# Gathering the 1/den sums and the second LN's ones matmuls into one block of column-tiled matmuls

## The chip, the cores and the metric

One NeuronCore of a Trainium2 chip runs the whole program. The metric is the device time of one execution in microseconds. Profiles are one execution each; their times count from the span's start, and the span is some 1.8 us shorter than the device time.

## The reference, cut to what matters

A conditioned transformer block: a layer norm with shift and scale, linear attention, a second layer norm with shift and scale, and a gated FFN. The change touches the denominator of the attention and the shift and scale of the second norm.

```python
mod = (_silu(c) @ w_mod).reshape(c.shape[0], 6, 1, -1)      # sa, ca, ga, sb, cb, gb
h = _layernorm(x) * (1 + ca) + sa
# linear attention, 32 heads of 32, 2048 tokens
z   = einsum('bhsd->bhd', pk)
num = einsum('bhqd,bhde->bhqe', pq, kv)
den = einsum('bhqd,bhd->bhq', pq, z)[..., None] + 1e-06
o   = num / den
x = x + ga * (o @ wo)
h = _layernorm(x) * (1 + cb) + sb                           # <- sb, cb
x = x + gb * (gelu(h @ w_gate) * (h @ w_up) @ w_down)
```

## The kernel before

The kernel records operations into one list per engine, with semaphores derived from the ranges they touch; VectorE, ScalarE and GpSimd are reordered by a small scheduler in one stretch, TensorE and the sync engine's transfers stay in program order.

The parts that matter: the denominator sums write 32 partitions each, four matmuls side by side; so do the ones matmuls that broadcast a row of modulation values.

```python
def den(pr_, b):                       # one token half: 8 groups x 4 column tiles
    for g in range(NG):
        for i in range(4):
            e.matmul(ps_all[32*i:32*(i+1), b*512:b*512+HW], Z32[:, g, :], PQ[sg][:, g, t0:t0+HW], ...)
    # VectorE: RDC = PSUM + 1e-6, RDC = 1/RDC;  store(): RDC -> scr_rd in HBM

def mod_pass():                        # second LN's shift and scale
    mod_rows(((2, 4, 5, hl_src),))     # 8 ones matmuls, 32 partitions each, into PSUM bank 5
    o_r = mod_store(4, 5, MROW[1], ...)            # ScalarE copy, store to scr_row in HBM
    for dst, nt, a0 in ((SBT, "sbT", 0), (CBT, "cbT", 2)):
        # load scr_row by column: 1024 elements of 4 bytes each
        e.dma_start(dst[:, :], scr_row[1, a0:a0+2, :].rearrange("a (b p) -> p (a b)", p=P))

# what runs after which key-times-x tile (m_tile) of the attention tail
HOOK = {..., 14: "w2 modp", 15: "kv3 z32", 16: "den0", 17: "w3", 18: "rb0.0",
        19: "kv4 den1", 20: "w4 rb0.1", ...}
```

1/den comes back from HBM as `rb`, broadcast over partitions, 1 MB for each half of a group of 512 tokens. Each chunk of 128 tokens is then normalised by ScalarE and GpSimd for the second norm (`ln2_a`: sum, squares, normalise) and transposed by a DMA.

```python
def xh_buf(c_):
    i = c_ % 3                         # three buffers: chunk 3 reuses chunk 0's
    return XH[i], r_2k(XHO[i], f"xh{i}")

for c_ in range(3, 12):
    ...
    if c_ == 4:
        pq_scale(1, 1, GH[0] + GH[1])
        rb_load(3, (0,))               # first half of the last reload, 1 MB
    wo_chunk(c_, 2 * (c_ % 4))
    ...
    if c_ in (4, 5, 6):
        ln2_a(c_ - 3, False)           # chunks 1 to 3, each with its transpose to h2T
```

## Time and profile before

| | before |
|---|---|
| device time, median of the 3 runs | 833.59 us (833.45 to 833.72) |
| TensorE busy | 99% of the span |
| first key-times-x tile starts | 126.97 us |
| first FFN matmul starts | 234.45 us |
| last addition starts | 829.47 us |

The last three rows are read from the timeline of TensorE and the chain by time (start, length, engine, line, what):

```profile
126.97 1.18 PE L826 MATMUL ps_all<-xrow,pk 128*128 128x341 bf16 x7
234.45 0.38 PE L1325 MATMUL ps_all<-h2T,wg 128*128 128x512 bf16 x1
829.47 0.22 DVE xall L1360
```

They cut the execution in three: a start-up of 127 us, a middle of 107.48 us that holds everything the change touches on TensorE, and an FFN of 595.02 us.

### The profile page before, as it was taken

The numbers are of one execution on the slowest core, as the hardware profiler recorded it, in microseconds if no ns is written. First come the engines' busy times: TensorE is split into PE (matmuls) and PEld (weight loads), VectorE is DVE, ScalarE is ACT, GpSimd is POOL, SyncE is SP. The second block draws the span as 40 slices with busy tenths as digits, with TensorE's granted clock in tenths as the row PEclk, the third lists the DMA queues.
The fourth block names the chain that finished last, engine by engine and source line by source line (L and its number), as shares of the span: only waits on it lengthen the run. The fifth ranks groups of instructions, "written<-read, shape, count | busy, mean of one in ns | idle before, by whom it ended". The sixth has DMA issues, their size and how long they took to land.

```text
span 831.7 us, 11593 instructions
## 1 busy us (share of the span) xinstructions
PE 826.5 (99%) x4253; PEld 392.3 (47%) x4253; DVE 509.9 (61%) x920; ACT 321.1 (39%) x542; POOL 35.5 (4%) x90
## 2 busy tenths in 40 slices
PE   8999999999999999999999999999999999999998
PEld 4444446665444444444444444444444444444445
DVE  6799888834777577753555565355556535555522
ACT  2597642323523354410444441044444104444300
POOL 2122100000200000000000000000000000000000
DMA  9798769368998788070555533055553306555000
GB/s 286 233 187 220 164 138 262 58 128 196 228 273 240 228 249 256 34 170 19 160 152 152 151 102 76 20 162 154 154 145 102 76 20 170 155 153 137 7 20 26
DMA packets 216929, 121.90 MB, mean 147 GB/s; under 512 B 69276, under 2 KB 206756, under 8 KB 215848
## 3 DMA queue, kind: packets, MB, share of 16 engines
q1 hardware_dynamic: 216856, 121.16, 55.9%
q8 instruction: 34, 0.56, 0.3%
q14 instruction: 23, 0.19, 0.1%
q10 hardware_dynamic: 16, 0.00, 0.0%
HBM read 103.03 MB, written 4.47 MB: 129 GB/s over the span
## 4 chain that ended last, share of the span: by engine, by line
PE 97%; SPq 2%; DMA 1%; issue 0%; DVE 0%
PE ps_all L1353 23%; PE ps_all L1328 23%; PE ps_all L1325 23%; PE ps_all L826 7%; PE ps_all L862 7%; PE ps_all L1189 7%; PE ps_all L811 5%; SPq L568 1%; DMA wmq<-in_w_mod_dram 1%; SPq L573 1%; PE ps_all L844 0%; PE ps_all L1121 0%; PE ps_all L1148 0%; SPq L562 0%; PE ps_all L771 0%
## 5 line engine op out<-in xcount | busy, mean ns | idle before, releaser
L1325 PE MATMUL ps_all<-h2T,wg 128*128 128x512 bf16 x896 | 339.6, 379 | 0.0
L1328 PE MATMUL ps_all<-h2T,wu 128*128 128x512 bf16 x896 | 339.6, 379 | 0.0
L1353 PE MATMUL ps_all<-wd,yT 128*128 128x512 bf16 (+3 forms) x952 | 194.2, 366 | 0.0
L1336 ACT ACTIVATE q<-ps_all 128x512 f32<-128x512 f32 x112 | 66.9, 597 | 224.4 <-PE ps_all L1325 223.2
L1353 PEld LDWEIGHTS ps_all<-wd,yT 128*128 128x128 bf16 x952 | 90.1, 98 | 103.7 <-issue 0.2
L1325 PEld LDWEIGHTS ps_all<-h2T,wg 128*128 128x128 bf16 x896 | 87.7, 98 | 105.7
L1328 PEld LDWEIGHTS ps_all<-h2T,wu 128*128 128x128 bf16 x896 | 87.7, 98 | 105.7
L1341 DVE SCALAR_TENSOR_TENSOR ww<-th,guh 128x512 f32<-128x512 f32 x112 | 77.5, 692 | 77.9 <-ACT th L1340 77.9
L1338 DVE SCALAR_TENSOR_TENSOR ww<-q,ps_all 128x512 f32<-128x512 f32 x112 | 77.0, 687 | 75.8 <-ACT guh L1337 75.7
L1340 ACT ACTIVATE th<-ww 128x512 f32<-128x512 f32 x112 | 70.5, 629 | 86.4 <-DVE ww L1338 86.4
L1358 DVE TENSOR_TENSOR ps_all<-ps_all,gbb 128x512 f32<-128x512 f32 (+3 forms) x34 | 22.7, 667 | 94.6 <-PE ps_all L1353 94.6
L1343 DVE TENSOR_TENSOR yT<-ww,ps_all 128x512 bf16<-128x512 f32 x112 | 76.9, 686 | 3.8
L1337 ACT ACTIVATE guh<-ps_all 128x512 f32<-128x512 f32 x112 | 66.2, 591 | 0.0
L811 PE MATMUL ps_all<-wk,h1T 128*128 128x512 bf16 x248 | 56.8, 379 | 0.4 <-DVE h1T L691 0.2
L862 PE MATMUL ps_all<-h1T,wq 128*128 128x512 bf16 x256 | 56.7, 379 | 0.0
L1189 PE MATMUL ps_all<-w,pq 128*128 128x512 bf16 x256 | 56.6, 379 | 0.0
L800 ACT ACTIVATE eb<-ps_all 128x512 f32<-128x512 f32 x64 | 36.2, 593 | 36.7 <-PE ps_all L811 13.9
L862 PEld LDWEIGHTS ps_all<-h1T,wq 128*128 128x128 bf16 x256 | 25.0, 98 | 29.9
L1189 PEld LDWEIGHTS ps_all<-w,pq 128*128 128x128 bf16 x256 | 24.9, 98 | 30.1 <-ACT w L1123 0.3
L811 PEld LDWEIGHTS ps_all<-wk,h1T 128*128 128x128 bf16 x248 | 23.7, 98 | 28.8 <-DVE h1T L691 2.3
L826 PE MATMUL ps_all<-xall,pk 128*128 128x342 bf16 (+1 forms) x216 | 35.3, 307 | 0.0
L630 ACT ACTIVATE xhd<-xall,nm,rs 128x1024 bf16<-128x1024 bf16 x12 | 14.9, 1240 | 38.2 <-DVE nm L620 31.7
(97 smaller groups left out, 508.3 us busy)
## 6 DMA issues: line engine op xcount, KB each, us to landing
wg<-in_B_w_gate_dram SPq DMA_DIRECT2D x56, 512.0 KB, 4.1
wu<-in_B_w_up_dram SPq DMA_DIRECT2D x56, 512.0 KB, 5.3
rb<-scr_rd SPq DMA_DIRECT2D x32, 256.0 KB, 6.5
wd<-in_B_w_down_dram SPq DMA_DIRECT2D x7, 1024.0 KB, 8.7
wmst<-in_w_mod_dram SPq DMA_DIRECT2D x6, 1024.0 KB, 6.2
wmq<-in_w_mod_dram SPq DMA_DIRECT2D x8, 512.0 KB, 6.7
out_dram<-xall SPq DMA_DIRECT2D x31, 128.0 KB, 1.7
xall<-in_A_x_dram SPq DMA_DIRECT2D x3, 1024.0 KB, 9.5
```

The source lines that it names most:

```text
L811: o = sch.op(T, lambda e, dc=dc: e.matmul(PS(bank), H1[sg][:, ci, dc, :], W_[:, dc, jg * 512:(jg + 1) * 512], start=(dc == 0), stop=(dc == ...
L826: o = sch.op(T, lambda e, c_=c_: e.matmul(PS(bank, 0, n), PK[c_][:, g * P:(g + 1) * P], xrow(c_, o_, o_ + n), start=(c_ == 0), stop=(c_ == ...
L862: o = sch.op(T, lambda e, dc=dc: e.matmul(PS(b), WQ[:, dc, qc * P:(qc + 1) * P], H1[sg][:, :, dc, :], start=(dc == 0), stop=(dc == NDC - 1 ...
L1189: last[half] = sch.op(T, lambda e, g=g, half=half: e.matmul(PS(b0 + half), PQ[sg][:, g, ci * P:(ci + 1) * P], W2[:, g, half * 512:(half + ...
L1325: og = sch.op(T, lambda e, dc=dc: e.matmul(PS(bg), WG[slot][:, dc, e_ * P:(e_ + 1) * P], H2[sg][:, dc, :], start=(dc == 0), stop=(dc == ND ...
L1328: ou = sch.op(T, lambda e, dc=dc: e.matmul(PS(bu), WU[slot][:, dc, e_ * P:(e_ + 1) * P], H2[sg][:, dc, :], start=(dc == 0), stop=(dc == ND ...
L1336: sch.op(A, lambda e: e.activation(Q1[j][:, :], PS(bg), ACTF.Square, scale=math.sqrt(GELU_A)), prd=pr(bg), wr=rq, note=f"q1 {fc}")
L1338: sch.op(V, lambda e: e.scalar_tensor_tensor(WW[j][:, :], Q1[j][:, :], 1.0, PS(bg), op0=ALU.add, op1=ALU.mult), rd=rq, prd=pr(bg), wr=rw, ...
L1340: sch.op(A, lambda e: e.activation(TH[j][:, :], WW[j][:, :], ACTF.Tanh, scale=GELU_C), rd=rw, wr=rt, note=f"th {fc}")
L1341: sch.op(V, lambda e: e.scalar_tensor_tensor(WW[j][:, :], TH[j][:, :], 1.0, GUH[j][:, :], op0=ALU.add, op1=ALU.mult), rd=rt + rg, wr=rw, n ...
L1343: sch.op(V, lambda e: e.tensor_tensor(YT[:, fc, :], WW[j][:, :], PS(bu), ALU.mult), rd=rw, prd=pr(bu), wr=r_yt(fc), note=f"yT {fc}")
L1353: o = sch.op(T, lambda e, b=b, fc=fc, c0=c0, c1=c1, n=n: e.matmul(PS(b, 0, n), YT[:, fc, ci * P:(ci + 1) * P], WDT[fc // 4][:, fc % 4, c0:c1],
```

## The change

Its intent: TensorE pays each time its stream goes from full-width matmuls to column-tiled ones and back. Before there are three column-tiled blocks in the attention tail; after there is one. To let them stand together, the second sums get PSUM bank 4 and a second 1/den buffer, and the ones matmuls bank 7. The two loads of the second norm's shift and scale are moved later on the sync engine's queue, and the first half of the last 1/den reload is moved behind three transposes.

```diff
-            ... ("rdc", [P, SGW // 2], f32, 1024),
+            ... ("rdc", [P, SGW // 2], f32, 1024), ("rdc1", [P, SGW // 2], f32, 1024),
 [...]
         def mod_pass():
-            mod_rows(((2, 4, 5, hl_src),))
-            o_r = mod_store(4, 5, MROW[1], r_2k(OFF_ROW + 2048, "mrow1"), 1)
+            mod_rows(((2, 4, 7, hl_src),))
+            return mod_store(4, 7, MROW[1], r_2k(OFF_ROW + 2048, "mrow1"), 1)
+
+        def col_loads(o_r):
             for dst, nt, a0 in ((SBT, "sbT", 0), (CBT, "cbT", 2)):
 [...]     # den(): RDC -> RDC[pr_]
-        HOOK = {..., 14: "w2 modp", 15: "kv3 z32", 16: "den0", 17: "w3", 18: "rb0.0",
-                19: "kv4 den1", 20: "w4 rb0.1", ...}
+        HOOK = {..., 14: "w2", 15: "kv3 z32", 16: "den0 den1 modp", 17: "w3", 18: "rb0.0",
+                19: "kv4", 20: "w4 rb0.1", ...}
 [...]
-                st[int(f[3:])] = den(int(f[3:]), 5)
+                st[int(f[3:])] = den(int(f[3:]), 5 - int(f[3:]))
 [...]
         st[1]()
+        col_loads(st["m"])
 [...]
             if c_ == 4:
                 pq_scale(1, 1, GH[0] + GH[1])
-                rb_load(3, (0,))
 [...]
             if c_ in (4, 5, 6):
                 ln2_a(c_ - 3, False)
+            if c_ == 6:
+                rb_load(3, (0,))
```

More of the change, by code (lines that the diff above doesn't have):

```diff
@@ L399, in bass_adaLN_cond__linear_attn_block__geglu_ffn__prompt_kernel @@
             ("ident", [P, P], bf16, 256), ("bmask", [P, P], bf16, 256), ("bm32", [P, NG, NH], bf16, 512),
-            ("z32", [P, NG, NH], bf16, 512), ("rdc", [P, SGW // 2], f32, 1024),
+            ("z32", [P, NG, NH], bf16, 512), ("rdc", [P, SGW // 2], f32, 1024), ("rdc1", [P, SGW // 2], f32, 1024),
             ("ones", [P, 32], bf16, 64), ("silf", [P, NDC], f32, 64),
@@ L414, in bass_adaLN_cond__linear_attn_block__geglu_ffn__prompt_kernel @@
         IDENT, BMASK, BM32, Z32 = (_small[k] for k in ("ident", "bmask", "bm32", "z32"))
-        RDC = _small["rdc"]
+        RDC = [_small["rdc"], _small["rdc1"]]
         ONES, SILF, C8, CT, CHALF, THC, SILUT = (_small[k] for k in ("ones", "silf", "c8", "cT", "chalf", "thc", "siluT"))
@@ L1141, in bass_adaLN_cond__linear_attn_block__geglu_ffn__prompt_kernel @@
         HW = SGW // 2
+        RN = ("rdc", "rdc1")
         def den(pr_, b):
@@ L1152, in den @@
             pset_writer(b, o)
-            sch.op(V, lambda e: e.tensor_scalar(RDC[:, :], PS(b, 0, HW), 1e-6, None, op0=ALU.add), prd=pr(b), wr=r_sm("rdc"), note=f"dene{pr_}")
-            sch.op(V, lambda e: e.reciprocal(RDC[:, :], RDC[:, :]), rd=r_sm("rdc"), wr=r_sm("rdc"), note=f"rden{pr_}")
+            sch.op(V, lambda e: e.tensor_scalar(RDC[pr_][:, :], PS(b, 0, HW), 1e-6, None, op0=ALU.add), prd=pr(b), wr=r_sm(RN[pr_]), note=f"dene{pr_}")
+            sch.op(V, lambda e: e.reciprocal(RDC[pr_][:, :], RDC[pr_][:, :]), rd=r_sm(RN[pr_]), wr=r_sm(RN[pr_]), note=f"rden{pr_}")
             def store():
-                o_rd[pr_] = sch.dma(Q, lambda e: e.dma_start(scr_rd[2 * pr_:2 * pr_ + 2].rearrange("s f k (g t) -> (s f k g) t", g=NG), RDC[:, :]),
-                          rd=r_sm("rdc"), note=f"rden{pr_}.st")
+                o_rd[pr_] = sch.dma(Q, lambda e: e.dma_start(scr_rd[2 * pr_:2 * pr_ + 2].rearrange("s f k (g t) -> (s f k g) t", g=NG), RDC[pr_][:, :]),
+                          rd=r_sm(RN[pr_]), note=f"rden{pr_}.st")
             return store
@@ L1202, in bass_adaLN_cond__linear_attn_block__geglu_ffn__prompt_kernel @@
         tiles = [(g, k) for g in range(4) for k in range(3)] + [(g, 0) for g in range(4, NG)] + [(g, k) for g in range(4, NG) for k in (1, 2)]
-        HOOK = {0: "ga", 6: "kv0", 8: "w0", 9: "kv1", 11: "w1", 12: "kv2", 14: "w2 modp", 15: "kv3 z32", 16: "den0", 17: "w3", 18: "rb0.0",
-                19: "kv4 den1", 20: "w4 rb0.1", 21: "", 22: "kv5", 23: ""}
+        HOOK = {0: "ga", 6: "kv0", 8: "w0", 9: "kv1", 11: "w1", 12: "kv2", 14: "w2", 15: "kv3 z32", 16: "den0 den1 modp", 17: "w3", 18: "rb0.0",
+                19: "kv4", 20: "w4 rb0.1", 21: "", 22: "kv5", 23: ""}
         st = {}
@@ L1212, in hook_run @@
             elif f == "modp":
-                mod_pass()
+                st["m"] = mod_pass()
             elif f == "z32":
```

## The prediction

> **What bounds the kernel now.** I read four views, in this order: the page's chain of work that ended last, the list of what TensorE waited for, the same chain in order of time around the tail of the attention block, and the sync engine's queue of transfers after it. The page first:
>
> ```profile
> span 831.7 us, 11593 instructions
> PE 826.5 (99%) x4253; PEld 392.3 (47%) x4253; DVE 509.9 (61%) x920; ACT 321.1 (39%) x542; POOL 35.5 (4%) x90
> ...
> PE 97%; SPq 2%; DMA 1%; issue 0%; DVE 0%
> ```
>
> TensorE makes up 97% of the chain that sets the end. Its busy share alone would not prove that, but the list of its waits does (waited for: us, times, longest):
>
> ```profile
> PE ps_all L598 <- POOL bmask L551: 2.1, 1, 2.1
> PE ps_all L811 <- DVE h1T L691: 0.2, 1, 0.2
> ```
>
> There are no others. From 26 us on, the end moves only if TensorE's own stream gets shorter or a new wait opens in it. The change rearranges 164 to 183 us. The chain there (start, length, what):
>
> ```profile
> 159.97 4.64 PE ps_all L826 x32
> 164.61 0.43 PE ps_all L1121 x2
> 165.04 0.55 PE ps_all L771 x8
> 165.59 2.43 PE ps_all L826 x16
> 168.01 0.45 PE ps_all L844 x8
> 168.46 2.32 PE ps_all L826 x16
> 170.78 0.99 PE ps_all L1148 x32
> 171.77 2.43 PE ps_all L826 x16
> ...
> 179.28 0.45 PE ps_all L844 x8
> 179.72 0.99 PE ps_all L1148 x32
> 180.71 2.43 PE ps_all L826 x16
> ```
>
> L826 x16 is one tile of the key-times-x product (16 matmuls of 341 or 342 columns); L844 (128 columns) and L1121 (512 columns) are full-width products between them. L771 x8 are the ones matmuls for the second LN's shift and scale; L1148 x32, twice, are the denominator sums. Both of these write 32 partitions per matmul, four side by side. The reader is to see the 2.32 against the 2.43: every key-times-x tile that follows a 32-wide block is 0.11 us longer than one that follows full-width work.
>
> Last, the sync engine's queue, because the change also moves transfers (start, time in the queue, what):
>
> ```profile
> 192.88 0.53 SPq L1156 DMA_DIRECT2D scr_rd<-rdc  x1
> 193.50 3.64 SPq L1168 DMA_DIRECT2D rb<-scr_rd  x8
> ...
> 219.22 2.18 SPq L1168 DMA_DIRECT2D rb<-scr_rd  x4
> 221.51 8.91 SPq L670 DMA_TRANSPOSE h2T<-xh  x3
> 230.52 0.53 SPq L1266 DMA_DIRECT2D wg<-in_B_w_gate_dram  x1
> ```
>
> It issues in order, so what is put ahead of a load makes that load later. In the issue view around 235 us, the gate and up weights of the third pair of FFN tiles land 12.3 and 13.4 us after issue, against 4.4 and 6.1 for the pair before: the queue is backed up there.
>
> **What the Trainium skill says.** "TensorEngine Tiling (Array Packing)", section Key Properties: "Mode switching requires drain: Changing tiling mode (not just tile) drains the TensorE". The trace agrees: the 0.11 us above, and as much on the way in (below). "TensorE: Matmul & The Clock Gate", Part 3 on packing small matmuls, says that matmuls in different tiles of the array run at the same time; 32 sums in 0.99 us are 8 rounds of four and nearly nothing else, so this agrees too. "DMA: Bandwidth & Descriptors", section Rules for kernel authors, says that a last dimension that isn't contiguous becomes one descriptor per element; the shift and scale loads show it: between 168 and 172 us 2082 packets moved 0.01 MB, landing 2.2 and 2.9 us after issue. The same page, section Queues, rings and completion order, has descriptors consumed in ring order on each DMA engine, so those loads delay what is behind them; no run here isolates that yet.
>
> **The change, part by part.** On TensorE no instruction is added or removed. Before there are three 32-wide blocks with full-width work around each: ones matmuls (after the third output-weight product), first sums, second sums three tiles later. After, the instruction order has first sums, second sums, ones matmuls back to back between two key-times-x tiles: one way in and one way out in place of three.
>
> Cost of one way in and out, from the chain. Column cadence: 342 columns take 2.32/16 = 0.145 us, 128 columns 0.45/8 = 0.056, so 0.00042 us a column and 0.109 us for 256. The sums: 8 rounds x 0.109 = 0.87 us; the piece is 0.99, so 0.12 is the way in. The tile after it: 2.43 - 2.32 = 0.11 for the way out. Together 0.23. The ones matmuls check it: 512 columns take 2.59/12 = 0.216 us (the twelve-matmul pieces of L1189 at 191 us), two rounds 0.43, piece 0.55, so 0.12 in; next tile 2.43, so 0.11 out. Three blocks now pay 0.69 us; one would pay 0.23. All of it lies on the chain. Saved: 0.46 us.
>
> The rest of the change is there to make this possible, and I expect it to cost TensorE nothing:
> - PSUM banks. The second sums go to bank 4, the ones matmuls to bank 7. Bank 4 was last read by a 0.28 us VectorE product that ended at 168.9; the second sums start near 171. Bank 7 was last read by ScalarE's copy of the output weights, done at 166.2; the ones matmuls start near 172. After the block, the next per-group product needs bank 4 back: VectorE has 0.42 + 1.75 + 0.42 us to run before that (the add, the reciprocal, the second add), 2.6 us, against 2.43 + 0.43 + 2 x 2.32 = 7.5 us of matmuls. The next output-weight product needs bank 7: ScalarE's row copy takes 0.59 us, against a 2.43 us tile.
> - A second buffer for 1/den. VectorE's two adds and two reciprocals keep their durations; its idle gaps there (3.2 and 5.5 us) hold them.
> - The shift and scale loads move from an idle queue at 168 us to just before the reload of 1/den for the second token group: about 1 us of issue (0.37 + 0.58), plus their packets. That reload lands near 200 us (first half; 4.7 after issue) and its first user starts at 205.25 on VectorE, so some 5 us of room.
> - The first half of the last 1/den reload (1 MB) moves behind the three h2T transposes, so it starts some 8 us later. Its user is VectorE at 235.66; I estimate landing at 234 to 237. VectorE has slack: its first FFN result frees its bank at 241.99, and the fourth FFN tile wants that bank at 244.8.
>
> Sum: 833.59 - 0.46 = 833.13; with an allowance for the rivals below I predict 833.2 us.
>
> **The rivals.**
> 1. The cost isn't the change of mode but a cost of any new accumulation group or bank, so a merged block pays the same 0.69 us and the time stays at 833.6. Against it: full-width groups also change bank and weights (L844 to L826 to L1121) and run at 2.32 and 0.43 with no extra. I give this 10%.
> 2. A new wait at the FFN's start. The moved 1 MB now stands closer ahead of the gate and up weights. Those of the third pair land at 235.18 + 12.3 = 247.5 and 235.73 + 13.4 = 249.1 us, and are needed at 251.7 and 251.9, which is 2.6 to 4 us of room (0.45 less after the gain). One MB at the roughly 250 GB/s seen there is 4 us. For it: the queue is full. Against it: the transposes, relieved of that traffic, should finish earlier and give time back, since the first two took 8.7 and 7.9 us to land and the third, less crowded, 3.3. If it happens, TensorE stalls 0.3 to 1.5 us once: 833.4 to 834.6. I give it 25%.
> 3. The 4-byte loads hold up the 1/den reloads by more than the 5 us of room, so the output-projection tiles of the second token group wait. That would need twice the 2.9 us they took to land before: 5%, some 1 us.
> 4. The gain is larger, because the shift of the first sums by 0.64 us (the ones matmuls are no longer before them) hastens the chain to the first 1/den reload. But TensorE never waits for that reload now, so this gains nothing.
>
> **Range and chances.** The three runs of before spread over 0.27 us (833.45 to 833.72), over half the expected gain. Without a stall I expect 832.9 to 833.4; with rival 2, up to 834.6. Eight in ten: 832.7 to 833.9. Two per cent would be 16.7 us, far beyond anything this touches: within 2% at 0.98, faster and slower 0.01 each.
>
> **What would show it.** Right, if in the chain by time a single run of L826 x16 follows the merged block at about 2.43 us and all others take 2.32; if the 72 narrow matmuls together take near 0.87 + 0.87 + 0.43 + 0.12 = 2.29 us; and if the FFN's first matmul comes 0.4 to 0.5 us earlier than 234.45. Step by step: rival 1 shows as extra time inside the block, above 2.4 us; rival 2 as a new line in TensorE's waits, or a gap, for gate or up weights near 251 us; rival 3 as a wait of VectorE for the reload near 205 us with TensorE stopping behind it. The prediction is wrong if the FFN starts earlier by that much and the end doesn't move: then the gain was given back later, and I would look at the transfers first.

## More of the kernel before

The ScalarE timeline around the fourth chunk of the second norm (chunk 3, counted from 0; start, length, engine, line, operation, then idle time before and what ended it), and GpSimd's small step between the two ScalarE passes:

```profile
220.44 1.04 ACT L638 ACTIVATE xh<-xall 128x1024 bf16<-128x1024 bf16 x1
...
224.52 1.24 ACT L630 ACTIVATE xh<-xall,nm,rs 128x1024 bf16<-128x1024 bf16 x1 [1.30 <-POOL nm L646]
```

```profile
221.73 0.22 POOL L639 TENSOR_SCALAR mv<-st 128x1 f32<-128x1 f32 x1 [2.47 <-ACT xh L638]
```

ScalarE's sum of the fourth chunk (L638) starts with no wait, and the normalised rows (L630) start at 224.52, which is 9.93 us before the first FFN matmul.

## The result, and the profile after

| | before | changed |
|---|---|---|
| device time, median of 6 runs each | 833.65 us (833.45 to 834.57) | 833.64 us (833.09 to 835.73) |
| ratio | | 1.0001, 95% interval 0.9988 to 1.0014 |

A ratio here is the mean time of one kernel's fast runs over that of the other's of the same rounds, so it isn't quite the ratio of the medians. The time is inside the predicted range, but the expected gain of half a microsecond isn't there. It is also far less than the interval can resolve, so from here on the traces decide.

First the merged block, in the chain by time of the changed kernel (start, length, what; L1152 are the sums, L771 the ones matmuls):

```profile
168.22 2.32 PE ps_all L826 x16
170.54 1.86 PE ps_all L1152 x64
172.40 0.43 PE ps_all L771 x8
172.83 2.43 PE ps_all L826 x16
```

The 72 narrow matmuls take 1.86 + 0.43 = 2.29 us, where the three blocks of before took 0.99 + 0.99 + 0.55 = 2.53. Only one tile of 2.43 us follows where there were three. The three marks of the changed kernel:

```profile
127.38 1.18 PE L826 MATMUL ps_all<-xrow,pk 128*128 128x341 bf16 x7
234.42 0.38 PE L1331 MATMUL ps_all<-h2T,wg 128*128 128x512 bf16 x1
830.04 0.23 DVE xall L1366
```

The middle, from the first key-times-x tile (127.38) to the first FFN matmul (234.42), is 107.04 us: 0.44 less than the 107.48 of before. So the block does what it was made for.

Now what TensorE waited for in the changed kernel, without the two waits that were there before:

```profile
PE ps_all L728 <- DMA wmq<-in_w_mod_dram: 0.5, 1, 0.5
PE ps_all L811 <- DMA wk<-in_A_wqkv_dram: 0.5, 1, 0.5
PE ps_all L1334 <- DMA wu<-in_B_w_up_dram: 0.4, 1, 0.4
```

Two are in the start-up, where TensorE's operations are the same in both kernels. The third is ours to explain: the up weights of the third pair of FFN tiles. In TensorE's timeline, a gate and an up matmul that normally start 0.22 us apart:

```profile
251.69 0.38 PE L1331 MATMUL ps_all<-h2T,wg 128*128 128x512 bf16 x1
252.49 0.39 PE L1334 MATMUL ps_all<-h2T,wu 128*128 128x512 bf16 x1 [0.42 <-DMA wu<-in_B_w_up_dram]
```

They start 0.80 us apart, so 0.6 us are lost (the 0.42 of the view counts from the modelled end of the matmul before). The FFN stretch, from 234.42 to the last addition at 830.04, is 595.62 us, 0.60 over before. Gain 0.44, loss 0.60.

Why do these weights come late? The sync engine's queue of the changed kernel (start, time in the queue, what):

```profile
193.43 0.44 SPq L1140 DMA_DIRECT2D sbT<-scr_row  x1
193.92 0.69 SPq L1140 DMA_DIRECT2D cbT<-scr_row  x1
...
210.98 4.18 SPq L670 DMA_TRANSPOSE h2T<-xh  x1
...
220.28 8.42 SPq L670 DMA_TRANSPOSE h2T<-xh  x3
228.79 1.94 SPq L1172 DMA_DIRECT2D rb<-scr_rd  x4
230.83 0.39 SPq L1271 DMA_DIRECT2D wg<-in_B_w_gate_dram  x1
...
238.58 5.05 SPq L1272 DMA_DIRECT2D wu<-in_B_w_up_dram  x1
```

The last row is the late load: issued at 238.58 (235.73 before), landed 13.9 us later at 252.5 (249.1 before). The same two places in the queue of before:

```profile
210.00 4.08 SPq L670 DMA_TRANSPOSE h2T<-xh  x1
...
235.73 4.42 SPq L1267 DMA_DIRECT2D wu<-in_B_w_up_dram  x1
```

The first transpose starts at 210.98, before at 210.00: that is the two small loads ahead of it, for in the runs below it starts 24.1 to 24.5 us before the first FFN matmul where these loads are early (runs 6, 7, 9 and 11), as before, and 22.6 to 23.4 where they are late (runs 1, 2, 4, 5, 10 and here). And the fourth transpose now ends the row of three at 228.7 though nothing stands in front of it any more. ScalarE and GpSimd show why:

```profile
221.42 1.06 ACT L638 ACTIVATE xh<-xall 128x1024 bf16<-128x1024 bf16 x1 [0.93 <-DMA h2T<-xh]
...
226.17 1.24 ACT L630 ACTIVATE xh<-xall,nm,rs 128x1024 bf16<-128x1024 bf16 x1 [1.51 <-POOL nm L646]
```

```profile
222.73 0.64 POOL L639 TENSOR_SCALAR mv<-st 128x1 f32<-128x1 f32 x1 [3.51 <-ACT xh L638]
```

The fourth chunk's sum now waits 0.93 us for a transpose, the first one, whose buffer it reuses. Before, that transpose landed 10.3 us after its issue, at 220.3, just ahead of the sum at 220.44; now it lands at 221.4.

The sum then meets a slow GpSimd step: 0.64 us for the 0.22 of before (a second small step, at 225.73, takes 0.41 for 0.19). VectorE is multiplying two SBUF tensors there, and the step ends 0.08 us after the multiply that it fell into (222.62 to 223.30). The Trainium skill, "GPSIMD Engine Reference", section Specifications, names contention with VectorE instructions of two SBUF inputs, which fits; no run isolates it. Overlap alone doesn't make the step slow: in run 1 it starts 0.13 us before the end of such a multiply and takes 0.22.

The fourth chunk's normalised rows start 8.25 us before the first FFN matmul in place of 9.93; of these 1.68 us, some 1.0 are the wait for the buffer and 0.7 the two slow steps. The transpose that needs them comes later, and the DMA engines have nothing to do meanwhile, because the 1 MB reload that used to fill this time now stands behind. The DMA line of the window 219 to 259 us, in 40 slices of 1 us (tenths busy), first before, then changed:

```profile
DMA  9999997999998799999999999999999999999999
```

```profile
DMA  9999999003996979999999899999999999999999
```

The zeros at 226 to 228 us are DMA time that before was in use.

This gives the theory in the form that stood at the end: the merged block saves 0.44 us; the two moved transfers together delay the third pair's weights beyond their use, and TensorE waits until they land. The expectations before runs 1 and 6 still put it all on the moved reload; that both moves are needed came out of run 6. Rivals: the cost isn't one of changing modes; one of the two moves alone makes the wait; the wait has to do with the block's earlier arrival and not with ScalarE's buffer; the changed kernel is slower in its start-up.

### The profile page after: what moved, and what is told of

Same layout as the page of the kernel before. It is cut to its first block, busy times and chain, and to the rows that moved or that the text cites. A ratio compares the mean times of both kernels' runs of the same rounds, so it can differ in the third digit from the quotient of the medians.

```text
span 832.2 us, 11518 instructions
## 1 busy us (share of the span) xinstructions
PE 821.7 (99%) x4179; PEld 391.9 (47%) x4253; DVE 509.7 (61%) x920; ACT 321.3 (39%) x542; POOL 36.2 (4%) x90
## 4 chain that ended last, share of the span: by engine, by line
PE 92%; SPq 3%; DMA 3%; issue 1%; DVE 1%; ACT 0%; ACTq 0%
PE ps_all L1359 23%; PE ps_all L1334 22%; PE ps_all L1331 21%; PE ps_all L826 7%; PE ps_all L862 7%; PE ps_all L811 5%; PE ps_all L1193 5%; DMA wu<-in_B_w_up_dram 2%; SPq L568 1%; DMA wmq<-in_w_mod_dram 1%; SPq L1172 1%; SPq L573 1%; PE ps_all L844 0%; PE ps_all L1121 0%; SPq L562 0%
## 5 line engine op out<-in xcount | busy, mean ns | idle before, releaser
L1331 PE MATMUL ps_all<-h2T,wg 128*128 128x512 bf16 x860 | 325.9, 379 | 0.0
L630 ACT ACTIVATE xhd<-xall,nm,rs 128x1024 bf16<-128x1024 bf16 x12 | 14.9, 1240 | 38.2 <-DVE nm L620 31.7
```

Source lines behind the costliest of these rows:

```text
L1331: og = sch.op(T, lambda e, dc=dc: e.matmul(PS(bg), WG[slot][:, dc, e_ * P:(e_ + 1) * P], H2[sg][:, dc, :], start=(dc == 0), stop=(dc == ND ...
```

## The experiments

Eleven runs in three sittings, each sitting on one chip, each run with 5 rounds. After the texts, all are put in one table.

**1. The reload early again.** The changed kernel with one move undone.

```diff
             if c_ == 4:
                 pq_scale(1, 1, GH[0] + GH[1])
+                rb_load(3, (0,))
 [...]
-            if c_ == 6:
-                rb_load(3, (0,))
```

> The changed kernel with one thing undone: the first half of the last 1/den reload stands again ahead of the three h2T transposes. Theory (the merged block saves 0.46 us and the moved reload gives it back as a wait for the third pair's up weights): no wait of TensorE near 252 us, those weights land by about 250.5, time 0.4 to 0.5 us under before, near 833.15. Rival A (merging saves nothing): same as before. Rival B (the late shift and scale loads alone bring the wait): wait stays, same as before.

Median 833.67 us against 833.76 for before; ratio 0.9998 (0.9986 to 1.0011). No wait of TensorE after the start-up. Middle 107.04, FFN 595.02: exactly the gain without the loss. The weights landed at 249.8 us. By the clock the expected 0.4 isn't visible in these five runs, which an interval of 0.13% each way doesn't allow anyway; the profiled execution had lost 0.58 us in the start-up. So the mechanism is shown, the time not yet.

**2. The blocks apart, the transfers moved.** The changed kernel with its three blocks put back where they were.

```diff
-        HOOK = {..., 14: "w2", 15: "kv3 z32", 16: "den0 den1 modp", ..., 19: "kv4", ...}
+        HOOK = {..., 14: "w2 modp", 15: "kv3 z32", 16: "den0", ..., 19: "kv4 den1", ...}
```

(with the sums and the ones matmuls in bank 5, as before)

> The changed kernel with the three 32-wide blocks where they stood before, so that only its transfers are moved. Theory: the end of the wait is set by the landing at about 252.5 us and not by TensorE, so TensorE arriving 0.46 us later waits only 0.1 to 0.3 us: time 0.1 to 0.3 us over before. If the wait were the same 0.6 us whatever the arrival, it would be 0.6 over before. Rival A (merging saves nothing, transfers harmless): same as before.

Median 833.82; ratio 1.0001 (0.9987 to 1.0014). Middle 107.48: no gain. FFN 595.34: a wait of 0.32 us, just over the expected 0.1 to 0.3. So the moved transfers make the wait without the merged block, and the rival of the block's earlier arrival falls. TensorE's up matmul starts within 0.05 us of the landing here (252.40) and in both profiles of the changed kernel (252.49; 251.87 in run 4): the landing sets the moment at which TensorE goes on. TensorE arrives 0.44 us later than with the merged block, but waits only 0.28 less than in the changed kernel's first profile and 0.07 less than in its second, because the landing itself isn't the same: 125.2 us after the first key-times-x tile here, 125.1 and 124.9 there. So an earlier arrival is spent in part on waiting.

**3. The second sums cut in eight.** The kernel before; each round of four sums stands between two pairs of matmuls of the next tile.

```diff
-            m_tile(g, k, n % 4, n % 2)
+            m_tile(g, k, n % 4, n % 2, (lambda r: den_round(1, 5, [r])) if n == 20 else None)
 # in m_tile, after every second matmul: cut(c_ // 2)
```

> The kernel before with the second sums cut into eight pieces of four matmuls, each between two pairs of matmuls of the next key-times-x tile: the same matmuls, seven more ways in and out. Theory (a cost of 0.23 us per way in and out): 7 x 0.23 = 1.6 us longer in that tile and, all of it on TensorE, 1.6 us over before in the end. Rival A (a cost per accumulation group or bank): no more groups, so within 0.1 us of before.

Median 835.37; ratio 1.0020 (1.0007 to 1.0033). The chain by time, start and end of the cut tile:

```profile
180.70 0.14 PE ps_all L826
180.84 0.22 PE ps_all L1152 x4
181.07 0.40 PE ps_all L826 x2
...
185.40 0.25 PE ps_all L826
185.65 0.43 PE ps_all L1123 x2
```

Four sums at a time cost one streaming of 256 columns, 0.109 us by the cadence in the prediction, yet each piece takes 0.22; and two matmuls of the tile, 0.29 us at 0.145 each, take 0.40. The sums and the tile together take 185.65 - 180.70 = 4.95 us; before they took 0.99 + 2.43 = 3.42. The difference, 1.53 us for seven more ways in and out, is 0.22 us each. The middle is 109.02 us, 1.54 over before, and the FFN 595.02. The number of accumulation groups and banks is unchanged, so the rival of a cost per group falls. What it is in the switch that takes the time, the draining of the array or the first weight load of the new mode, no run separates.

**4. The changed kernel again**, beside the others.

> The changed kernel once more, beside the others on one chip. Theory: a wait of TensorE for the third pair's up weights near 252 us of 0.4 to 0.8 us again, the merged block again near 2.3 us, time within 0.3 us of before and 0.4 to 0.6 over the one with the early reload. If the wait seen once was chance, it is absent and the time is 0.4 under before.

Median 833.76; ratio 0.9999 (0.9986 to 1.0011). Middle 107.04, and the wait is back, smaller:

```profile
251.87 0.39 PE L1334 MATMUL ps_all<-h2T,wu 128*128 128x512 bf16 x1 [0.21 <-DMA wu<-in_B_w_up_dram]
```

FFN 595.41, a loss of 0.39 us. That is at the lower edge of what was expected for the wait. Against run 1 the traces show the 0.39; the medians differ by 0.09, which these runs don't resolve. The wait is no chance, though its size varies.

**5. The x tiles behind the weights.** The changed kernel with another 1 MB load out of the way.

```diff
                 rb_load(3, (1,))
-                x_dma(12, 16)
 [...]
         stream_pair(0, 2)
+        x_dma(12, 16)
```

> The changed kernel with the 1 MB load of the last x tiles issued behind the third pair of gate and up weights in place of ahead of it. Theory: those weights land about 4 us earlier (near 248.5 us), TensorE doesn't wait for them, the merged block keeps its gain: first key-times-x tile to first FFN matmul 107.04 us, from there to the last addition 595.02 (the value without a wait). Rival (something else than the landing of these weights holds TensorE there): 595.4 or more. Risk: the x tiles now land near 252.5 and are used near 254.

Median 833.71; ratio 0.9994 (0.9981 to 1.0008). Middle 107.03, FFN 595.02, no wait. The up weights landed at 250.8 us in an execution whose FFN began at 235.46, 15.3 us after its start; 2.8 us were won, less than the 4 expected. It is the landing that holds TensorE, and nothing else there.

**6. Only the reload late.** The kernel before with this one move of the change.

```diff
             if c_ == 4:
                 pq_scale(1, 1, GH[0] + GH[1])
-                rb_load(3, (0,))
 [...]
+            if c_ == 6:
+                rb_load(3, (0,))
```

> The kernel before with only the 1/den reload moved behind the transposes; blocks and the shift and scale loads where they were. Theory (this move alone makes the wait, as the transposes wait for ScalarE meanwhile and the DMA engines idle): wait as with the blocks apart, 107.48 and 595.3 us. Rival (the shift and scale loads are half of the delay): no wait, 107.48 and 595.0.

Median 834.12; ratio 1.0006 (0.9993 to 1.0018). Middle 107.47, FFN 595.02: no wait. My theory missed here: this move alone doesn't make the wait. The weights landed 15.7 us after the first FFN matmul, 1.0 later than before, and the limit is 17.5. Its clock time came out above before with no step of the trace to answer for it, inside the interval; I don't explain it. With run 1, where the small loads alone were late (15.2, or 0.5 later), the two moves separately cost 1.5 us of room; together they cost 3.4 (3.1 in run 4). This compares kernels with and without the merged block. With the block in all of them, counted from run 11 (13.9), the small loads cost 1.3 (run 1), the reload 2.1 (run 9), both together 4.2 or 3.9. Two profiles of one kernel differ by 0.2 to 0.3. So they cost more together than apart, but by how much stays open.

**7. The shift and scale loads at once.** Run 1's kernel, with these loads right after the merged block.

```diff
-                st["m"] = mod_pass()
+                col_loads(mod_pass())
 [...]
-        col_loads(st["m"])
```

> The changed kernel with the early reload, and the shift and scale loads issued right after the merged block in place of late. Theory of why they were moved: they wait some 2 us for their row's store on the in-order queue, the next transpose of the key-times-x rows starts 1.5 to 2.5 us later and TensorE's next per-group product near 180 us waits 0.5 to 1.5 us: 107.5 to 108.5 us to the first FFN matmul, eating the gain of the block. Rival (the queue has room): 107.04.

Median 833.91; ratio 1.0001 (0.9988 to 1.0014). The queue and TensorE's wait:

```profile
174.52 0.54 SPq L780 DMA_DIRECT2D scr_row<-mrow  x1
176.23 0.37 SPq L1140 DMA_DIRECT2D sbT<-scr_row  x1
176.64 0.58 SPq L1140 DMA_DIRECT2D cbT<-scr_row  x1
177.39 1.48 SPq L670 DMA_TRANSPOSE mtb<-mb  x1
```

```profile
PE ps_all L844 <- DMA mtb<-mb: 0.3, 1, 0.3
```

The loads wait for the store of their row, and the transpose that the next per-group product needs goes out at 177.39, in run 1 at 175.95. The middle is 107.59, 0.55 over run 1: the whole gain of the block is gone. So on the sync engine's queue the loads could not simply stand right behind the block. That they had to go as far back as the change put them is not shown: run 9 has them early on another queue.

**8. The kernel before, against itself.**

> The kernel before, unchanged, against itself. The stretches are to come out as before: 107.48 and 595.02 us, within 0.1; the time from the start to the first key-times-x tile is to vary as it did between runs (126.97 to 128 us), if the start is what makes executions differ by up to 1 us. If the start is constant for this kernel, the changed kernel's start would be slower by itself.

Median 833.81; ratio 1.0001 (0.9988 to 1.0013). Middle 107.48, FFN 595.02, as in the first profile. The first key-times-x tile started at 127.46, 0.49 us later than in the first profile of the same kernel, with waits on start-up loads that the first one didn't have. So the start-up varies by itself, and it is what makes executions of one kernel differ.

**9. The shift and scale loads from ScalarE's queue**, the reload late as in the change.

```diff
-                sch.dma(Q, lambda e, dst=dst, a0=a0: e.dma_start(dst[:, :], scr_row[1, ...
+                sch.dma(A, lambda e, dst=dst, a0=a0: e.dma_start(dst[:, :], scr_row[1, ...
 # called after tile 20 ("w4 cols rb0.1"), not after st[1]()
```

> The changed kernel with the two shift and scale loads issued from ScalarE's queue at about 177 us in place of the sync engine's at 193; the late reload kept. Theory (these two loads hold up the first h2T transpose, whose buffer the fourth chunk's sum on ScalarE waits for, and only together with the late reload does that reach TensorE): ScalarE no longer waits for the transpose, the third pair's up weights land about 16 us after the first FFN matmul (18.1 in the changed kernel, needed at 17.5), stretches 107.04 and 595.02 us. Rival (the late loads don't matter, the shift comes from the block): wait stays, 595.4 to 595.6.

Median 833.25 against 833.82; ratio 0.9993 (0.9979 to 1.0006). Middle 107.05, FFN 595.02, no wait; the weights landed 16.0 us after the first FFN matmul, and ScalarE doesn't wait for a transpose.

**10. A buffer of its own for the fourth chunk.** All transfers as the change put them.

```diff
-                b_, rng = xh_buf(c_)
+                b_, rng = xh_buf(c_) if c_ != 3 else (XHD[0], r_2k(OFF_ROW, "xhd0"))
```

> The changed kernel with a buffer of its own for the fourth chunk's normalised rows, so that ScalarE's sum there need not wait for the first transpose; all transfers where the change put them. Theory (that wait of 0.8 to 0.9 us is the link from the late loads to the late weights): ScalarE's wait is gone, the last transpose and everything behind it come 1 us or more earlier, no wait of TensorE, 107.04 and 595.02. Rival (the queue itself is late, whatever ScalarE does): wait of 0.3 us or more remains, 595.3 to 595.6.

Median 833.25; ratio 0.9994 (0.9982 to 1.0007). ScalarE's timeline:

```profile
220.22 1.04 ACT L638 ACTIVATE xhd<-xall 128x1024 bf16<-128x1024 bf16 x1
...
224.29 1.24 ACT L630 ACTIVATE xhd<-xall,nm,rs 128x1024 bf16<-128x1024 bf16 x1 [1.30 <-POOL nm L646]
```

The wait before L638 is gone, and the normalised rows start 9.94 us before the first FFN matmul (234.23), as before the change. The weights land 16.0 us after it. Middle 107.04, FFN 595.02. This edit moves no transfer in the queue; it changes only what the fourth sum has to wait for (the GpSimd step behind it is back at 0.22 us as well). So the buffer's reuse is the link between the late small loads and the late weights.

**11. All early.** Run 9 with the reload early, the version with the most room.

> The merged block with the shift and scale loads on ScalarE's queue and the reload early again: the version with the most room. Theory: 107.04 and 595.02 us, weights landing 14.7 us after the first FFN matmul as in the kernel before. By the clock 0.44 under before, beneath what 5 rounds resolve; pooled with the other versions without a wait (early reload, x tiles behind, loads on ScalarE, fourth buffer) 0.2 to 0.5 under. Rival (start-up slower in the changed kernels): the pooled time equals before.

Median 833.39; ratio 0.9993 (0.9981 to 1.0006). Middle 107.07, FFN 595.02. The weights landed 13.9 us after the first FFN matmul, 0.8 earlier than expected.

**All in one table.** Middle = first FFN matmul less first key-times-x tile; FFN = last addition less first FFN matmul; landing = issue plus time to landing of the third pair's up weights less first FFN matmul (needed at 17.5). In us, from each run's profile.

| | start-up | middle | FFN | landing |
|---|---|---|---|---|
| before, first profile | 126.97 | 107.48 | 595.02 | 14.7 |
| 8 before again | 127.46 | 107.48 | 595.02 | 14.9 |
| changed, first profile | 127.38 | 107.04 | 595.62 | 18.1 |
| 4 changed again | 126.97 | 107.04 | 595.41 | 17.8 |
| 1 reload early | 127.55 | 107.04 | 595.02 | 15.2 |
| 2 blocks apart | 127.13 | 107.48 | 595.34 | 17.8 |
| 3 sums cut | 127.95 | 109.02 | 595.02 | 14.4 |
| 5 x tiles behind | 128.43 | 107.03 | 595.02 | 15.3 |
| 6 only reload late | 127.38 | 107.47 | 595.02 | 15.7 |
| 7 loads at once | 127.36 | 107.59 | 595.02 | 14.5 |
| 9 loads on ScalarE | 127.30 | 107.05 | 595.02 | 16.0 |
| 10 fourth buffer | 127.19 | 107.04 | 595.02 | 16.0 |
| 11 all early | 127.78 | 107.07 | 595.02 | 13.9 |

Every merged version has a middle of 107.03 to 107.07 except run 7, every one with the three blocks whole and apart 107.47 or 107.48, and the FFN is longer only where the landing is past 17.5.

**The clock.** Five versions have the merged block and no wait (runs 1, 5, 9, 10, 11). The mean of their 25 timed runs is 833.47 us; the mean of the 38 runs of before in all rounds, run 8's included, is 833.84; that of the changed kernel's 11 is 833.81. The standard errors, from the spread of the single runs, are 0.08, 0.07 and 0.21. So without the wait the gain is 0.38 us, 0.05%, give or take 0.10, in agreement with the 0.44 of the traces; with the wait the changed kernel and before can't be told apart. The runs come from several sittings and not all from the same rounds. Within the sittings, the five are 0.15 (run 1), 0.26 (run 5) and 0.49 us (runs 9 to 11) under before, with standard errors of 0.19, 0.28 and 0.19; weighted by runs 0.37, give or take 0.13. So the clock agrees, but most of its weight comes from one sitting. No version can be called best among the five; run 10 is the least edit to the change, run 11 has the most room.

## Why the prediction was right or wrong

- **What bounds the kernel, and the cost of a change of mode**: right. 0.46 us were predicted for the block, 0.44 were found in the middle stretch, and 0.41 to 0.45 in the six other merged profiles but run 7's. The narrow matmuls took 2.29 us as worked out, and a single tile of 2.43 followed. Cutting the sums in eight gave 0.22 us per way in and out against the predicted 0.23.
- **Rival 1 (a cost per group or bank)**, given 10%: wrong; run 3 refutes it.
- **Rivals 3 and 4**: neither showed. VectorE's first use of the second token group's reload started at 205.22 (205.25 before), so the small loads did not hold up that reload beyond its room. The chain to the first reload was not hastened either: its first user waited 3.03 us and started at 184.15 (183.52 before), which, as expected, TensorE didn't feel.
- **PSUM banks and the second buffer cost nothing**: right; no wait on VectorE or ScalarE for them shows on TensorE in any run.
- **The step that failed** is the sum "833.59 - 0.46 = 833.13" with its estimate that the moved transfers cost TensorE nothing. Rival 2, given 25%, is what happened: a new line in TensorE's waits, for up weights, near 252 us. The size stated for it, "0.3 to 1.5 us once", holds (0.60, 0.39 and, with the blocks apart, 0.32). The time lies in the range, but only because the allowance for this rival made it wide; as a forecast of the time, the sum was half a microsecond off, all of the gain.
- **The mechanism given for rival 2 was half of it.** I took the moved 1 MB as the cause. Alone it uses 1.0 us of the room and makes no wait (run 6). The other half I had looked at and cleared: "some 5 us of room" for the shift and scale loads. That followed them only to the reload right behind them, which indeed lost nothing. It didn't follow them on to the first h2T transpose behind the reloads, whose landing frees a buffer for ScalarE. Runs 9 and 10 show that link from both its ends. Two small slips changed nothing: the room is 251.7 - 247.5 and 251.9 - 249.1, so 4.2 and 2.8 us, not "2.6 to 4", and the reload's start moved by 9.6 us (219.22 to 228.79), not "some 8".
- **"The transposes, relieved of that traffic, should finish earlier and give time back"**: wrong for the changed kernel. The last of them is held by ScalarE's rows and not by traffic, so taking the 1 MB from ahead of it left the DMA engines idle for 2 us.
- **The last reload's landing at 234 to 237 us and VectorE's room**: right. VectorE waited for it until 236.44 (1.80 us), with no harm to TensorE.
- **Spread of the runs**: understated. The 0.27 us of three runs of before became 1.1 us in six. The start-up alone gave 126.97 to 128.43 us in these profiles.

Still open: why the wait is 0.60 in one profile of the changed kernel and 0.39 in the other. The landings relative to the start of the FFN differ by 0.3 us; the cause of that wasn't looked for.

## What to carry to other kernels

Count the ways in and out of a tiled mode in a stream that TensorE bounds: here each pair costs 0.22 us, and blocks of 4 to 72 narrow matmuls each paid it once. A gain of half a microsecond ahead of a load that barely makes it is only kept if the load is moved forward too, so write down the room of each transfer behind the edit before counting the gain. Follow a moved transfer past its next neighbour, to every buffer that its delay keeps busy. And when the effect is below the spread of the clock, cut the trace at two marks that all versions share and compare the stretches.

## What the Trainium skill lacked or had wrong

- "TensorEngine Tiling (Array Packing)", Key Properties, says that a change of mode drains TensorE but gives no cost. Here going from 128-column to 32-column tiles and back cost 0.22 us (1.53 us for seven pairs), about half on each side, and sums and ones matmuls of different groups, banks and widths stood in one block without paying it (2.29 us for 72 matmuls, equal to their streaming time and one way in).
- No page that I read gives the variation of a start-up that waits for many loads: the first key-times-x tile began between 126.97 and 128.43 us over 13 profiles, with the same TensorE operations ahead of it.
